# Two more PSUM banks for the products of the first two f-pairs' gate in moe2's first 512-token block

## The chip, the cores and the metric

The kernel runs on one core of a Trainium2 chip. The metric is the device time of one execution in microseconds (us); the lower the better. The work is spread over five engines with a queue each: TensorE (PE) multiplies, VectorE (DVE), ScalarE (ACT) and GpSimd (POOL) do the elementwise work, SyncE (SP) issues the DMA transfers. PE writes into PSUM, which has eight banks per partition; a bank holds 512 fp32 values. Before PE may overwrite a bank, the engine that reads the old result out of it must be done.

## What is computed

Three layers, one after the other. First, attention with a window of 128 positions, 4 batches of 8 heads, 576 positions each, 64 wide. Then two feed-forward layers on the 2304 tokens of width 512:

```python
def _moe_ref(x, w_in, w_out):          # d_ff 2048
    h = x @ w_in
    r = np.maximum(h, 0.0)
    return ((r * r) @ w_out)

def _moe2_ref(x, w_gate, w_val, w_out):  # d_ff 1536
    gate = 1.0 / (1.0 + np.exp(-(x @ w_gate)))
    val = x @ w_val
    return (gate * val @ w_out)
```

The weights come as 64-bit floats and the result is fp32. To keep the precision, each operand is split into a high and a low part of type fp32r, and a product is made of three matmuls: high by high, high by low, low by high.

## The kernel before

The kernel first lists all its operations with what each reads and writes (`plan.op`), then a planner (`Plan.schedule`) plays the list through with a cost for each operation on each engine it may run on. The order in which the planner starts the operations is the order in which they are written into the five queues. Each engine then works through its queue strictly in that order, and an instruction waits until what it depends on is done. Where an operation may run on DVE or POOL (`dve_or_pool`, line 375), the planner also chooses the engine. Buffers are slots in groups; the eight PSUM banks are the group `b`. A buffer gets its bank when its first operation is planned, and the bank comes free when the last operation that uses the buffer is done. So one operation that may start earlier or later in the plan moves all that follow it, on all engines, up to the end.

The last layer, moe2, goes over the tokens in five blocks: block 0 of 256 tokens, and blocks 1 to 4 of 512 tokens each. Block 0 is computed directly: `gv` (lines 1033 to 1035) makes gate and val into the banks `pg` and `pv`, and `o_step` (line 1062) multiplies by `w_out` into the banks `o`.

Blocks 1 to 4 use a Strassen-Winograd scheme with seven products instead of eight. For each pair of 128-wide slices of d_ff (f = 0, 2, 4, 6, 8, 10) and each of gate and val, `gv_strassen` makes the seven products P1, P2, P6, P7, P5, P4, P3, each of six matmuls of 256 columns (line 937). I call these seven products a part; a block has twelve parts: gate 0, val 0, gate 2, val 2, and so on. All parts share two PSUM buffers: P1, P6, P5 and P3 go to `pa`, and P2, P7 and P4 go to `pd`. Before the next product may go to the same bank, its result is taken out:

- P1, P6 and P5 by an ACT copy into `cg` (line 338), P7 by an ACT copy into `qc` (line 338);
- P2 and P4 by a DVE addition onto `cg` (line 953);
- P3 by an ACT sigmoid for gate (line 971), by a DVE multiplication for val (line 982).

The result of a val part is then multiplied with the gate, combined into sums (`ss`, line 995) and split into high and low parts `ah` (ACT at line 338, DVE or POOL at line 335). From these, `o_strassen` (line 1095) makes the products of the output layer, six of them into six banks `o`, in groups of three matmuls; the seventh goes through `pd` (line 1095 as well, out by line 1113). Two such calls per f-pair are spread over the parts that follow. The weights of the parts are fetched from a scratch area in HBM by SP: the tiles that hold sums (`st2`, shown as st) have five buffers, and each part needs four of them.

`xb` (called per block) loads the tokens of a block into `xf`, makes four sums of them (DVE or POOL), and splits the seven operands into high parts (ACT, line 338) and low parts (DVE, line 335).

Of the kernel before, what the change touches and what calls it, by code (L numbers as in the profile page):

```python
# [287 lines left out]
def attention_moe_moe2_kernel(ctx: ExitStack, tc, q, k, v, w_in, w_out1, w_gate, w_val, w_out2, out):  # L288
# [26 lines left out]
    TOP = {k: "t" for k in ("tq", "tk", "ts", "tp", "tv")}  # L315
    CAP = {"raw": 3, "nq": 1, "nk": 1, "qs": 1, "ks": 1, "wt": 6, "vs": 3, "st": 4, "pt": 2, "t": 3,
           "h": 2, "y": 4, "pg": 2, "pv": 2, "o": 6, "pa": 1, "pd": 1, "xacc": 2, "ob": 2, "ysg": 2, "raw2": 2, "pp": 2, "xp": 2,
           "tg": 2, "tw": 2, "st2": 5, "so": 5, "xf": 6, "cg": 4, "ss": 2, "ah": 12, "oc": 4, "qc": 3}
    CAP0 = {"nat": 2, "nq": 4, "nk": 4, "qs": 3, "qw": 3, "ks": 3, "vs": 3, "st": 5, "pt": 6, "t": 6}
    plan = Plan(SIZE, TOP)  # L320
# [3 lines left out]
    def new(kind, shape, dtype, early=False):  # L324
        g = GROUP[kind]
        t = TOP.get(kind, kind)
        cap = CAP0.get(t, CAP.get(t)) if early else CAP.get(t)
        return plan.buf(kind, g, cap, lambda slot: pools["ps" if g == "b" else "sb"].tile(
            shape, dtype, tag="%s%d" % (g, slot), name=kind, bufs=1))
# [588 lines left out]
    PAD = {}  # L918
    LATER = 2.0

    def gv_strassen(n, kind, f, e0):
        where, wts = XB[n], TW.pop((n, kind, f))
        for k in ("pa", "pd"):
            if k not in PAD:
                PAD[k] = new(k, [128, 512], F32)
        kA, kD = PAD["pa"], PAD["pd"]
        A, D = (lambda: kA()[:, :256]), (lambda: kD()[:, :256])

        def product(name, ps, start=False):
# [253 lines left out]
    for n in range(nblk):  # L1183
        e0 = endA + 3 * F2 * n
        xb(n, e0 - (14 if n == 0 else 3))
        for f in range(F2):
            e1 = e0 + 3.0 * f
            if n == 0:
                gv(n, f, e1)
                if f:  # L1190
                    o_step(0, f - 1, e1)
                continue
            if (n, f) == (1, 0):
                o_step(0, F2 - 1, e1)

            if todo and todo[0][0] <= (n - 1) * F2 + f:
                o_strassen(*todo.pop(0)[1:], e1)
            kind, f0 = ("gate", "val")[f % 2], f // 2 * 2
            sums(n, kind, f0, e1 - 9)
            gv_strassen(n, kind, f0, e1)  # L1200
            if f % 2:
                sums(n, "out2", f0, e1 - 6)
                todo += [((n - 1) * F2 + f + 2 + i, n, f0, i) for i in range(2)]
# [52 lines left out]
```

## Time and profile before

| what | value |
|---|---|
| three timed runs | 985.03, 985.9, 986.41 us, median 985.9 us |
| the profiled execution | 986.72 us, of which the span from first to last instruction is 985.0 us |
| PE busy | 963.0 us (98% of the span), 7676 matmuls |
| DVE, ACT, POOL busy | 625.0, 568.4, 218.0 us |
| mean granted TensorE clock | 0.997 of full speed |

A busy PE is not PE at its fastest. The end of a matmul is modelled (0.28 us after its start), while the next matmul starts 0.12 us after it in a dense stretch. A pause of up to 0.16 us between two matmuls is therefore still shown as busy. What PE loses is better read from the start times in the timeline, or from the number of matmuls in a stretch of fixed length, than from the busy share.

### The profile page before, as it was taken

What the parts mean: (1) busy time and instruction counts of PE and PEld (TensorE: products, weight loads), DVE (VectorE), ACT (ScalarE), POOL (GpSimd) and SP (SyncE); (2) the same over time, 40 slices, a digit from 0 to 9 for tenths busy, and PEclk for the clock granted to TensorE, in tenths of its full rate; (3) what the DMA queues carried; (4) which work ended last, traced back from release to release, by engine and by line L of the source; (5) the groups of instructions that cost most, each with busy time, mean ns of one, the idle gap of its engine ahead of it and who ended that gap; (6) DMA issues with size and microseconds to landing.
All of it is one profiled execution on the core that took longest, in us unless ns stands there. A gap on an engine that the chain in (4) does not pass through costs nothing.

```text
span 985.0 us, 21787 instructions
## 1 busy us (share of the span) xinstructions
PE 963.0 (98%) x7676; PEld 911.5 (93%) x7676; DVE 625.0 (63%) x1630; ACT 568.4 (58%) x1536; POOL 218.0 (22%) x339
## 2 busy tenths in 40 slices
PE   7899999999999999999999999999999999999997
PEld 6599989998988998998899999899999999999997
DVE  6999988777687777567621324536755485565555
ACT  7887777776677587576643423444544444454433
POOL 4611112314232223114200001102221141122121
PEclk9999999999999999999999999999999999999999
DMA  8645558656784776675689741676776677677931
GB/s 227 148 146 166 172 150 257 201 170 193 227 239 152 240 245 203 197 211 179 205 280 358 255 120 37 183 215 204 234 264 215 216 247 250 200 232 258 333 117 44
DMA packets 188140, 201.71 MB, mean 205 GB/s; under 512 B 86400, under 2 KB 119680, under 8 KB 188032
## 3 DMA queue, kind: packets, MB, share of 16 engines
q1 hardware_dynamic: 188032, 200.33, 65.0%
q8 instruction: 61, 1.00, 0.4%
q14 instruction: 47, 0.39, 0.1%
HBM read 153.09 MB, written 47.19 MB: 203 GB/s over the span
## 4 chain that ended last, share of the span: by engine, by line
PE 83%; DMA 5%; ACT 5%; DVE 4%; issue 3%; POOL 1%; SPq 0%; POOLq 0%; DVEq 0%; ACTq 0%
PE y L818 18%; PE pa L937 13%; PE pd L937 10%; PE o L1095 10%; PE h L781 6%; PE h L783 6%; PE h L782 6%; PE tv L759 3%; DMA wscr<-pp 2%; DMA raw<-in_moe_w_in_dram 2%; PE ts L637 2%; PE pd L1095 2%; PE o L1062 1%; PE tp L726 1%; PE tq L602 1%
## 5 line engine op out<-in xcount | busy, mean ns | idle before, releaser
L818 PE MATMUL y<-gs,wh 128*128 128x256 f32 (+1 forms) x1024 | 217.4, 304 | 0.0
L818 PEld LDWEIGHTS y<-gs,wh 128*128 128x128 f32 x1024 | 163.6, 190 | 9.1 <-issue 7.3
L781 PE MATMUL h<-x,wh 128*128 128x256 f32 (+1 forms) x512 | 156.2, 305 | 0.4 <-ACT qs L607 0.4
L783 PE MATMUL h<-x,wl 128*128 128x256 f32 (+1 forms) x512 | 151.2, 295 | 0.4 <-DVE wl L335 0.4
L818 PE MATMUL y<-gs,wl 128*128 128x256 f32 (+1 forms) x512 | 151.4, 296 | 0.0
L782 PE MATMUL h<-x,wh 128*128 128x256 f32 (+1 forms) x512 | 151.0, 295 | 0.0
L338 ACT ACTIVATE cg<-pa 128x256 f32<-128x256 f32 x144 | 55.1, 383 | 110.8 <-PE pa L937 94.3
L335 DVE TENSOR_TENSOR gs<-r,gs 128x320 fp32r<-128x320 f32 (+1 forms) x121 | 57.3, 473 | 74.9 <-ACT gs L338 74.6
L736 POOL TENSOR_SCALAR_AFFINE_SELECT pt<-pt 128x256 f32<-128x256 f32 (+1 forms) x144 | 67.6, 490 | 164.9 <-ACT pt L730 139.9
L781 PEld LDWEIGHTS h<-x,wh 128*128 128x128 f32 x512 | 96.7, 189 | 3.4 <-issue 2.1
L783 PEld LDWEIGHTS h<-x,wl 128*128 128x128 f32 x512 | 96.5, 188 | 0.6 <-DVE wl L335 0.6
L818 PEld LDWEIGHTS y<-gs,wl 128*128 128x128 f32 x512 | 96.9, 189 | 0.0
L782 PEld LDWEIGHTS h<-x,wh 128*128 128x128 f32 x512 | 96.6, 189 | 0.0
L795 ACT ACTIVATE r<-h 128x256 f32<-128x256 f32 (+1 forms) x128 | 51.9, 406 | 73.6 <-PE h L783 72.5
L937 PE MATMUL pa<-x,st 128*128 128x256 f32 x576 | 85.0, 283 | 1.1 <-ACT cg L338 1.0
L953 DVE TENSOR_TENSOR cg<-cg,pd 128x256 f32<-128x256 f32 x96 | 40.0, 416 | 62.9 <-ACT cg L338 58.1
L937 PEld LDWEIGHTS pa<-x,st 128*128 128x128 f32 x576 | 74.8, 189 | 1.8 <-ACT cg L338 1.7
L995 POOL TENSOR_TENSOR ss<-cg 128x256 f32<-128x256 f32 x31 | 27.4, 885 | 192.6 <-DVE cg L982 75.5
L1095 PE MATMUL o<-wr,ah 128*128 128x256 f32 x432 | 69.0, 281 | 0.2 <-DVE ah L335 0.2
L1095 PE MATMUL o<-so,ah 128*128 128x256 f32 x432 | 66.2, 281 | 0.0
L667 ACT ACTIVATE st<-st,sm 128x128 f32<-128x128 f32 x144 | 56.7, 402 | 13.4 <-DVE sm L660 13.3
L338 ACT ACTIVATE gs<-r 128x256 fp32r<-128x256 f32 (+1 forms) x128 | 56.4, 441 | 8.5 <-PE y L818 4.5
(175 smaller groups left out, 2139.7 us busy)
## 6 DMA issues: line engine op xcount, KB each, us to landing
st<-wscr SPq DMA_DIRECT2D x192, 256.0 KB, 3.9
wscr<-pp SPq DMA_DIRECT2D x72, 512.0 KB, 3.6
so<-wscr SPq DMA_DIRECT2D x96, 256.0 KB, 3.9
raw<-in_moe_w_out_dram SPq DMA_DIRECT2D x28, 512.0 KB, 4.0
wr<-wscr SPq DMA_DIRECT2D x54, 256.0 KB, 4.9
raw<-in_moe_w_in_dram SPq DMA_DIRECT2D x16, 512.0 KB, 4.8
raw<-in_moe_w_gate_dram SPq DMA_DIRECT2D x12, 512.0 KB, 4.6
raw<-in_moe_w_val_dram SPq DMA_DIRECT2D x12, 512.0 KB, 4.3
```

The lines of the kernel that those rows point to most:

```text
L335: return lambda e: eng(e).tensor_tensor(out=out(), in0=a(), in1=b(), op=ALU.subtract)
L338: return lambda e: nc.scalar.activation(out=out(), in_=in_(), func=AF.Copy, scale=scale)
L667: op({"ACT": 386}, lambda e, x=x: nc.scalar.activation(out=st()[:, x, :], in_=st()[:, x, :], func=AF.Exp, bias=sm()[:, x:x + 1], scale=-1. ...
L736: op({"POOL": pool_sel(2 * cols)}, lambda e: nc.gpsimd.affine_select(out=pt_of(what, j), in_=pt_of("own", j), pattern=[[0, 2], [1 if mine ...
L781: nc.tensor.matmul(ps()[:, :N], w[0]()[:, c], x()[:, 0, cc, :N], start=cc == 0, stop=False)
L782: nc.tensor.matmul(ps()[:, :N], w[0]()[:, c], x()[:, 1, cc, :N], start=False, stop=False)
L783: nc.tensor.matmul(ps()[:, :N], w[1]()[:, c], x()[:, 0, cc, :N], start=False, stop=cc == CC - 1)
L795: op({"ACT": act_ns(N, True)}, lambda e: nc.scalar.activation(out=g()[:, :N], in_=ps()[:, :N], func=AF.Relu), r=[ps], w=[g], prio=ep, also ...
L818: nc.tensor.matmul(y()[:, c0:c0 + N], w[a]()[:, c], gs()[:, b, :N], start=f == 0 and p == 0 and n != 1, stop=f == F1 - 1 and p == 2, skip_ ...
L937: nc.tensor.matmul(ps()[:, :256], w()[:, z * 256 + cc * 128:z * 256 + cc * 128 + 128], x, start=start and cc == 0 and i == 0, stop=cc == 1 ...
L953: op({"DVE": dve_ns(256)} if psum else dve_or_pool(256), lambda e: eng(e).tensor_tensor(out=quarter(i, j)(), in0=quarter(i, j)(), in1=src( ...
L1095: nc.tensor.matmul(o()[:, 256 * t:256 * t + 256], a_()[:, c_ + 128 * t:c_ + 128 * t + 128], w()[:, 256 * z:256 * z + 256], start=start and ...
```

## The change

In block 1 the parts are numbered 0 (gate 0), 1 (val 0), 2 (gate 2), 3 (val 2) and so on. Parts 0 and 2 write their products to two new PSUM buffers `pa2` and `pd2`; all other parts of block 1, and blocks 2 to 4, use `pa` and `pd` as before.

```diff
-             "h": "b", ..., "o": "b", "pa": "b", "pd": "b"}
+             "h": "b", ..., "o": "b", "pa": "b", "pd": "b", "pa2": "b", "pd2": "b"}
...
-           "h": 2, "y": 4, "pg": 2, "pv": 2, "o": 6, "pa": 1, "pd": 1, "xacc": 2, ...
+           "h": 2, "y": 4, "pg": 2, "pv": 2, "o": 6, "pa": 1, "pd": 1, "pa2": 1, "pd2": 1, "xacc": 2, ...
...
     def gv_strassen(n, kind, f, e0):
         where, wts = XB[n], TW.pop((n, kind, f))
-        for k in ("pa", "pd"):
+
+        ka, kd = ("pa", "pd") if n > 1 or 2 * (f // 2) + (kind == "val") not in (0, 2) else ("pa2", "pd2")
+        for k in (ka, kd):
             if k not in PAD:
                 PAD[k] = new(k, [128, 512], F32)
-        kA, kD = PAD["pa"], PAD["pd"]
+        kA, kD = PAD[ka], PAD[kd]
```

No instruction of the computation is added or removed. The two new buffers take two of the eight banks from the end of block 0 until the last product of part 2 has been read; then the banks go to `o`. The number of matmuls stays. The order of all queues is the same up to the first product of block 1 and differs from there to the end of the program. On POOL the order holds 225 rows before and 204 after, on DVE 1518 and 1540; of the splits into `ah` that are 512 wide, POOL has 4 before and 23 after.

The first place is PE in the middle of parts 0 and 1 of block 1. Before, from P4 of gate 0 on:

```order
L937 MATMUL pd<-xp,st_8129 128x256 x6
L937 MATMUL pa<-xp,wr 128x256 x6
L937 MATMUL pd<-x,wr 128x256 x6
L937 MATMUL pa<-x,wr 128x256 x6
L937 MATMUL pa<-x,st_8245 128x256 x6
L937 MATMUL pd<-x,st_8731 128x256 x6
L937 MATMUL pa<-x,st_8754 128x256 x6
L937 MATMUL pd<-xp,st_8766 128x256 x6
L937 MATMUL pa<-xp,wr 128x256 x6
```

These are P4 and P3 of gate 0, then P2, P1, P6, P7, P5, P4, P3 of val 0. P6 (the fifth row) goes to the same bank as P1 right ahead of it. Now the same place, from P3 of gate 0 on; `pa_8694` and `pd_8702` are the new buffers `pa2` and `pd2`, `pa` and `pd` without a number the old ones, and L939 is the former L937:

```order
L939 MATMUL pa_8694<-xp,wr 128x256 x6
L939 MATMUL pd<-x,wr 128x256 x6
L939 MATMUL pa<-x,st_8245 128x256 x6
L939 MATMUL pa_8694<-x,wr 128x256 x6
L939 MATMUL pd<-x,st_8740 128x256 x6
L939 MATMUL pa<-x,st_8753 128x256 x6
L939 MATMUL pd_8702<-x,wr 128x256 x6
L939 MATMUL pd<-xp,st_8774 128x256 x6
L939 MATMUL pa<-xp,wr 128x256 x6
L939 MATMUL pd<-x,wr 128x256 x6
L939 MATMUL pa<-x,wr 128x256 x6
```

Rows 2, 3, 5, 6, 8 and 9 are P2, P6, P7, P5, P4 and P3 of val 0; P1 of val 0 stands further up, as the third product of the block. Rows 4 and 7 are P1 and P2 of gate 2, and the last two rows P2 and P1 of val 2. The products of two or three parts are interleaved.

The second place is PE at the start of block 2. Before, from the seventh output product of a pair (`pd<-so,ah`) to P3 of gate 0 of block 2 and the output products behind it:

```order
L1095 MATMUL pd<-so,ah 128x256 x6
L1095 MATMUL o<-wr,ah 128x256 x3
L937 MATMUL pa<-x,wr 128x256 x6
L937 MATMUL pd<-x,wr 128x256 x6
L937 MATMUL pa<-x,st_9743 128x256 x6
L937 MATMUL pd<-x,st_9796 128x256 x6
L937 MATMUL pa<-x,st_9803 128x256 x6
L937 MATMUL pd<-xp,st_9822 128x256 x6
L1095 MATMUL o<-wr,ah 128x256 x9
L937 MATMUL pd<-x,wr 128x256 x6
L937 MATMUL pa<-xp,wr 128x256 x6
L1095 MATMUL o<-wr,ah 128x256 x3
```

The third row is P1 of block 2, and P2, P6, P7, P5, P4 follow with no output product between them; behind the nine output products stand P2 of val 0 and P3 of gate 0, and the next product to `pa`, P1 of val 0, stands right behind the last row. Now, from P1 of block 2 on:

```order
L939 MATMUL pa<-x,wr 128x256 x6
L1097 MATMUL o<-so,ah 128x256 x9
L939 MATMUL pa<-x,st_9757 128x256 x6
L1097 MATMUL o<-so,ah 128x256 x3
L1097 MATMUL pd<-so,ah 128x256 x6
L1097 MATMUL o<-wr,ah 128x256 x3
L939 MATMUL pa<-x,st_9794 128x256 x6
L1097 MATMUL o<-wr,ah 128x256 x3
L939 MATMUL pd<-x,wr 128x256 x6
L939 MATMUL pa<-xp,wr 128x256 x6
L1097 MATMUL o<-wr,ah 128x256 x3
L939 MATMUL pd<-x,st_9763 128x256 x6
```

P1, P6 and P5 now stand ahead of P2, with output products between them, and P3 and P7 follow. The products that go to `pa` run ahead of those that go to `pd` from block 1's third pair to the end.

## Rows read from the trace of the kernel before

**Rows 1.** The page: busy time by engine, and the chain that ended last
```profile
PE 963.0 (98%) x7676; PEld 911.5 (93%) x7676; DVE 625.0 (63%) x1630; ACT 568.4 (58%) x1536; POOL 218.0 (22%) x339
...
PE 83%; DMA 5%; ACT 5%; DVE 4%; issue 3%; POOL 1%; SPq 0%; POOLq 0%; DVEq 0%; ACTq 0%
```

**Rows 2.** Stretches of 20 us: busy us and (x instructions) per engine, clock, DMA
```profile
610.00:630.00 20.00, 17.77 (x140) 16.73 (x139) 12.64 (x23) 9.33 (x23) 4.73 (x5) 1.00 0.51 159
640.00:660.00 20.00, 20.00 (x171) 20.00 (x171) 9.02 (x20) 8.52 (x21) 2.25 (x3) 1.00 0.69 202
...
700.00:720.00 20.00, 19.16 (x155) 18.48 (x154) 16.30 (x31) 9.26 (x22) 8.01 (x9) 1.00 0.71 239
...
780.00:800.00 20.00, 19.15 (x160) 18.74 (x158) 14.04 (x25) 11.50 (x27) 6.07 (x5) 1.00 0.77 247
800.00:820.00 20.00, 19.99 (x168) 19.75 (x167) 12.48 (x24) 7.69 (x19) 6.49 (x8) 1.00 0.90 284
...
880.00:900.00 20.00, 18.62 (x154) 18.15 (x153) 15.14 (x27) 9.30 (x22) 9.79 (x9) 1.00 0.63 203
900.00:920.00 20.00, 20.00 (x170) 19.95 (x169) 10.89 (x23) 10.02 (x24) 3.39 (x4) 1.00 1.02 373
```

**Rows 3.** Waits of PE from 608 us on: total us, times, longest
```profile
PE pd L937 <- DVE cg L953: 3.9, 5, 1.3
PE pa L937 <- ACT cg L338: 1.0, 2, 0.5
PE o L1095 <- DVE ah L335: 0.2, 1, 0.2
```

**Rows 4.** Timeline, first block: start, us, engine, line [idle before <-releaser]
```profile
614.25 1.35 POOL L335 TENSOR_TENSOR xf<-xf 128x512 f32<-128x512 f32 x1 [3.92 <-PE o L1062]
614.37 1.78 DVE L335 TENSOR_TENSOR xf<-xf 128x512 f32<-128x512 f32 x1
...
614.69 0.88 PE L937 MATMUL pa<-xp,wr 128*128 128x256 f32 x6
...
616.08 0.41 DVE L953 TENSOR_TENSOR cg<-cg,pd 128x256 f32<-128x256 f32 x1
...
616.53 0.98 PE L937 MATMUL pd<-x,wr 128*128 128x256 f32 x6 [0.97 <-DVE cg L953]
...
617.35 0.88 PE L937 MATMUL pa<-x,wr 128*128 128x256 f32 x6
618.27 0.38 ACT L338 ACTIVATE cg<-pa 128x256 f32<-128x256 f32 x1 [1.12 <-PE pa L937]
...
618.71 0.97 PE L937 MATMUL pa<-x,st 128*128 128x256 f32 x6 [0.47 <-ACT cg L338]
```

**Rows 5.** Timeline of PE at the start of block 2
```profile
700.00 0.90 PE L937 MATMUL pa<-x,st 128*128 128x256 f32 x6
701.60 0.97 PE L937 MATMUL pd<-x,st 128*128 128x256 f32 x6 [0.70 <-DVE cg L953]
702.40 0.89 PE L937 MATMUL pa<-x,st 128*128 128x256 f32 x6
...
705.63 0.87 PE L937 MATMUL pa<-xp,wr 128*128 128x256 f32 x6
706.33 0.51 PE L1095 MATMUL o<-wr,ah 128*128 128x256 f32 x3
706.97 0.97 PE L937 MATMUL pa<-x,wr 128*128 128x256 f32 x6
```

**Rows 6.** Timeline: a wide multiplication on DVE, a wide split on POOL
```profile
635.98 0.69 DVE L982 TENSOR_TENSOR cg<-cg 128x512 f32<-128x512 f32 x1
...
914.99 1.29 POOL L335 TENSOR_TENSOR ah<-ss,ah 128x512 fp32r<-128x512 f32 x1 [2.10 <-DMA so<-wscr]
```

**Rows 7.** DMA issues from 600 to 640 us: count, KB each, median us to landing
```profile
st<-wscr SPq DMA_DIRECT2D x14, 256.0 KB, 3.0
```

More of the change, by code (lines that the diff above doesn't have):

```diff
@@ L313, in attention_moe_moe2_kernel @@
              "xf": "s", "xacc": "s", "cg": "s", "ss": "s", "ah": "s", "ysg": "s", "oc": "s", "qc": "r",
[1 row of a table removed]
[1 row of a table added]
     TOP = {k: "t" for k in ("tq", "tk", "ts", "tp", "tv")}
     CAP = {"raw": 3, "nq": 1, "nk": 1, "qs": 1, "ks": 1, "wt": 6, "vs": 3, "st": 4, "pt": 2, "t": 3,
-           "h": 2, "y": 4, "pg": 2, "pv": 2, "o": 6, "pa": 1, "pd": 1, "xacc": 2, "ob": 2, "ysg": 2, "raw2": 2, "pp": 2, "xp": 2,
+           "h": 2, "y": 4, "pg": 2, "pv": 2, "o": 6, "pa": 1, "pd": 1, "pa2": 1, "pd2": 1, "xacc": 2, "ob": 2, "ysg": 2, "raw2": 2, "pp": 2, "xp": 2,
            "tg": 2, "tw": 2, "st2": 5, "so": 5, "xf": 6, "cg": 4, "ss": 2, "ah": 12, "oc": 4, "qc": 3}
```

2 rows, old and new, of the table GROUP are left out of this document.

## The prediction

> **What bounds the kernel now.** I read the page first [rows 1]: PE is busy for 98% of the span, and 83% of the chain that ended last is PE. So only what PE itself does or waits for counts. The clock is at full speed in the stretches that matter (the column behind POOL reads 1.00 in [rows 2], the higher of its two levels, 2.4 GHz), so it is no term here.
>
> The busy share hides short pauses, since the modelled end of a matmul lies 0.28 us after its start. So next I counted matmuls in stretches of 20 us over blocks 1 to 4 [rows 2]. A clean stretch holds 171 (640 to 660), which is 20 / 171 = 0.117 us for a matmul. Five stretches hold fewer: 140 at the start of block 1, 155 at the start of block 2, 160 and 168 at that of block 3, 154 at that of block 4. The deficits are 31 + 16 + 11 + 3 + 17 = 78 matmuls, and 78 x 0.117 = 9.1 us. The rest of the four blocks runs at 170 to 172 in a stretch.
>
> Then the waits [rows 3]: what PE waits for is nearly always a bank. For `pd` it is the DVE addition that takes out P2 or P4, for `pa` the ACT copy. No transfer is among them.
>
> The timeline shows the price of a bank that is reused too soon. A group of six matmuls takes 0.71 us from start to next start. At 617.35 P1 goes to `pa`, and P6 right behind it goes to `pa` too [rows 4]: P6 starts at 618.71, 1.36 us later instead of 0.71. The steps are 0.88 until the last matmul is through, 0.04 to the start of the ACT copy, 0.38 for the copy, 0.06 to PE. So a bank is free again about 0.65 us after PE could have gone on, and with a DVE addition (0.41, [rows 4]) 0.69. After a wait, the first group needs 0.82 instead of 0.71 (616.53 to 617.35), which is 0.10 more for each wait.
>
> From this follows a rule to read an order by: count the matmuls that stand between two products in the same bank. Six (0.71 us) just cover the reading; three (0.355) leave 0.30, with the restart 0.4; none leaves 0.65, with the restart 0.75. The case of three is in [rows 5]: P3 to `pa` at 705.63, three output matmuls at 706.33, the next product to `pa` at 706.97 instead of 706.68. And six are enough only while DVE or ACT come at once. At 616.53 and 701.60 they did not: P2 waited 1.84 - 0.71 = 1.13 us [rows 4], and P7 of block 2 waited 1.60 - 0.71 = 0.89 [rows 5]. In the first case DVE sat 1.78 us in one subtraction, which POOL's subtraction, begun 0.12 us earlier, held up; the addition came only behind it, at 616.08.
>
> **The change, step by step.** The new banks themselves cost nothing: no matmul, copy or addition is added. `pa2` and `pd2` take two banks that `pg` and `pv` have left, and give them back before the six `o` banks are all wanted.
>
> What counts is the order, and in it the distance between products in one bank. In the whole PE order before, of 358 such pairs 2 have none between them, 4 have three and 37 have six; the others have nine or more. In the new order, of 356 pairs none has less than six, 8 have six, the others nine or more. The reason is the alternation that the order shows: a product to `pa`, three output matmuls, a product to `pd`. It begins in block 1 because two parts can be under way at once, and the planner keeps it to the end, because `pa` runs ahead and `pd` behind. With `pd` behind, the copy that the DVE addition adds onto is always there when the product is done.
>
> Terms of the gain, against the profiled execution of 986.72 us:
> - All deficits of the five stretches: 9.1 us. To this I add the fourth pair with three between, which lies in the last block's last part (0.4). Together 9.5 us that could go. In it are the two pairs with none (2 x 0.75 = 1.5) and the four with three (4 x 0.4 = 1.6), which the order removes for certain; the other 6.4 us are waits at distances of six or more, where DVE or ACT came late.
> - What comes back for certain: in block 1, P3 of val 0 is followed by P2 of val 2 and then by P1 of val 2 to the same bank. P3 of a val part is read by a DVE multiplication, and the DVE order puts P4's addition and the 512-wide multiplication (0.69, [rows 6]) ahead of it. From the end of P4 that is 0.21 + 0.41 + 0.69 + 0.41 + 0.06 = 1.78 us, and PE has P3 and P2 to do, 1.42. Left are 0.36, with the restart 0.46.
> - One pair in `pd` with six between is read by DVE (P4 of val 0, then P2 of val 2): between 0 and 1.23 us, what the same pair costs before (1.13 and 0.10). It is nearer to the lower end, since the addition has no POOL subtraction ahead of it; I take 0.3.
> - The three starts of a block. DVE has its burst of splits there as before. Between P4 of the old part, the seventh output product and P2 of the new block there is now room, so the wait of 0.89 + 0.10 = 1.0 has no place of its own, but other additions follow at a distance of nine, with 0.38 us to spare. Between 0 and 1.0 for each; with nothing nearer, I take the middle, 3 x 0.5 = 1.5.
> - The end of the program: the last output products wait for the last split in both orders, with the same 24 matmuls between. Nothing changes.
>
> Sum: 9.5 - 0.46 - 0.3 - 1.5 = 7.2 us. The execution of 986.72 becomes 979.5; the median of the three runs is 0.8 lower than that execution, so I predict 985.9 - 7.2 = 978.7. With the lower bounds of what comes back (0 for all) it is 976.4, with the upper ones (0.46 + 1.23 + 3.0 = 4.7, a gain of 4.8) 981.1.
>
> **Rivals.**
> - The gain ends with block 1. The waits at the three block starts may come from DVE's burst of splits (16.3 of 20 us busy at 700 to 720, [rows 2]) and not from the distance; then they come back in the new order at another product. Only the first stretch gains: 31 x 0.117 - 0.46 - 0.3 = 2.9, so 983.0. For it speaks that the distance there was six, where in other places six cost nothing; against it that the order has no six there any more.
> - Slower, through POOL. Of the splits into `ah` that are 512 wide, 23 go to POOL instead of 4. One holds POOL for 1.29 us [rows 6], and a DVE subtraction that meets it waits it out, as at 614.37 [rows 4]; an addition queued behind it then keeps `pd`. If each meeting costs 1.23, six of the 19 new ones eat up the gain of 7.2, and ten make 12.3 - 7.2 = 5.1 more, 991.0. For it: the one clear meeting in [rows 4]. Against it: the split at 914.99 lies in a stretch of 170 matmuls [rows 2, 6], so it cost PE nothing, and in POOL's order most of the new ones stand between the block starts.
> - No change, since something else holds PE at the same pace. Three parts under way want their weights sooner, through five buffers. P5 of val 0 can be fetched once P7 of gate 0 is done, after five groups, and is needed after fourteen: 9 x 0.71 = 6.4 us for a fetch that lands after 3.0 [rows 7]. At 900 to 920 the DMA queues are full (share 1.02), and PE still does 170 matmuls [rows 2]. If transfers took back all of it, the time would stay at 985.9. The Trainium skill (TensorE: Matmul & The Clock Gate, HAM oscillation — how this bites in real kernels) reports of a kernel whose loop had been reordered that "Adding PSUM double-buffering gave no further gain". By that rule nothing would change here either and the time would be 985.9; the trace does not bear it out, since here PE's waits name the bank's reader [rows 3].
>
> **How the numbers follow.** Forecast 0.76, gain ends with block 1 0.12, no change 0.07, slower through POOL 0.05. The forecast's own range is 976.4 to 981.1. To leave out no more than 2 in 10 I take in the first rival: 976.4 to 983.2. About 0.2%, or 2 us, is what a measurement of this kernel can tell from no change. The forecast lies beyond that with its whole range, the first rival mostly (0.11 of 0.12). So faster 0.87, same 0.08, slower 0.05.
>
> **What would show it.** In the changed kernel's trace: the stretch of 20 us from the first product of block 1 should hold 160 matmuls or more, and those at the block starts 166 or more. The waits of PE for DVE's addition should fall from 3.9 us to about 1. One wait of about 0.4 us should stand ahead of P1 of val 2 in block 1. Waits of PE for `st` tiles would show the third rival right, stretches of fewer than 165 matmuls in the middle of blocks beside wide POOL splits the second. The prediction is wrong in its main step if the block starts still miss more than ten matmuls each.

## The result, and the profile after

| | kernel before | changed kernel |
|---|---|---|
| timed, median (lowest to highest) | 986.15 us (985.03 to 987.03) | 976.04 us (975.76 to 976.71) |
| ratio to before | | 0.9907, 95% interval 0.9894 to 0.992 |
| timed again beside other kernels | 985.74 us | 975.63 us, ratio 0.9901 (0.9885 to 0.9917) |
| profiled execution, its span | 986.72, 985.0 us | 976.05, 974.3 us |

The change saves 10.1 us by the medians, 9.2 by the ratio. Forecast were 978.7 us and a gain of 7.2, with a range from 976.4 to 983.2. The sign and, in the main, the mechanism fit the numbers below; the gain was forecast 2 to 3 us too small, and the median of 976.04 lies 0.4 us beyond the range's lower end (the ratio on the 985.9 us shown before gives 976.7, just inside).

Of the profiled difference of 10.7 us, 1.0 has nothing to do with the change. Up to the first product of block 1 the order is the same in both kernels, and yet this product starts at 608.69 before and at 607.68 after. In the profiles of all the kernels below, it starts between 605.74 and 608.69. So from here on I compare the time from the first product of block 1 to the last group of output matmuls, both read from the timeline of one execution. I call it the PE stretch. First the timeline of the kernel before (start, us, engine, line, operation):

```profile
608.69 0.88 PE L937 MATMUL pa<-x,wr 128*128 128x256 f32 x6
...
978.50 0.86 PE L1095 MATMUL o<-wr,ah 128*128 128x256 f32 x6
```

And that of the changed kernel:

```profile
607.68 0.88 PE L939 MATMUL pa<-x,wr 128*128 128x256 f32 x6
...
967.80 0.87 PE L1097 MATMUL o<-wr,ah 128*128 128x256 f32 x6
```

That is 369.81 and 360.12 us: the change is worth 9.69 us. The changed kernel's profile from the second timed comparison gives 360.12 again, so this measure repeats far better than the time of a whole execution. Of the kernel before there is one profile.

The page after, which answers to [rows 1]: PE does the same 7676 matmuls and has a larger share of the chain that ended last (91% instead of 83%).

```profile
PE 959.1 (98%) x7676; PEld 910.7 (93%) x7676; DVE 626.7 (64%) x1653; ACT 571.0 (59%) x1537; POOL 205.0 (21%) x315
...
PE 91%; DVE 3%; ACT 2%; DMA 1%; issue 1%; SPq 0%; POOL 0%; POOLq 0%; DVEq 0%; ACTq 0%
```

PE's busy time fell by only 3.9 us of the 10, since up to 0.16 us of each pause counts as busy. The matmuls per stretch tell more; the stretches after that answer to [rows 2]:

```profile
610.00:630.00 20.00, 19.84 (x165) 19.48 (x163) 11.40 (x23) 11.36 (x28) 3.83 (x5) 1.00 0.57 172
...
700.00:720.00 20.00, 20.00 (x170) 20.00 (x169) 14.60 (x28) 9.46 (x23) 6.67 (x6) 1.00 0.75 237
...
780.00:800.00 20.00, 20.00 (x172) 20.00 (x171) 16.82 (x31) 10.05 (x24) 8.43 (x9) 1.00 0.86 277
800.00:820.00 20.00, 20.00 (x170) 20.00 (x170) 11.91 (x25) 9.68 (x24) 3.01 (x3) 1.00 0.76 249
...
880.00:900.00 20.00, 20.00 (x170) 20.00 (x169) 12.20 (x25) 8.16 (x20) 5.88 (x6) 1.00 0.84 272
```

Where 140, 155, 160, 168 and 154 matmuls stood, there are now 165, 170, 172, 170 and 170. At 780 to 800 DVE is busy for 16.82 of 20 us, and PE runs without a gap. (The stretches lie at fixed times, and the changed kernel reaches block 3 some 5 us sooner: before, the same burst of DVE shows in the stretch from 790 to 810, with 17.44.) Of PE's waits [rows 3], the 3.9 us for DVE's addition and the 1.0 us for ACT's copy are gone; these two are left:

```profile
PE o L1097 <- DVE ah L335: 0.2, 1, 0.2
PE pa L939 <- DVE cg L984: 0.2, 1, 0.2
```

The second is the predicted wait ahead of P1 of val 2. In the timeline after, from P3 of val 0 on:

```profile
619.99 0.88 PE L939 MATMUL pa<-xp,wr 128*128 128x256 f32 x6
...
620.71 0.94 PE L939 MATMUL pd<-x,wr 128*128 128x256 f32 x6
620.72 0.69 DVE L984 TENSOR_TENSOR cg<-cg 128x512 f32<-128x512 f32 x1
621.33 0.42 DVE L984 TENSOR_TENSOR cg<-pa,cg 128x256 f32<-128x256 f32 x1
...
621.80 0.98 PE L939 MATMUL pa<-x,wr 128*128 128x256 f32 x6 [0.16 <-DVE cg L984]
...
622.62 0.88 PE L939 MATMUL pa<-x,st 128*128 128x256 f32 x6
```

P2 starts at 620.71, 0.72 after P3: no wait ahead of it, though its six matmuls take 0.94 instead of 0.88, 0.06 more. P1 starts 1.09 after P2 instead of 0.71, and the group behind it 0.82 later: 0.38 + 0.11 = 0.49 us, of which 0.06 is P2's own and 0.43 the wait of P1, where 0.46 was forecast. The view of waits shows 0.2 of that, because it counts from the modelled end of the matmul before.

Why the starts of blocks cost nothing shows at block 2. First the kernel before, ahead of the rows of [rows 5]: POOL's subtraction, two splits of the new block's operands on DVE, P2 of gate 0, and the addition that reads it:

```profile
698.77 1.28 POOL L335 TENSOR_TENSOR xf<-xf 128x512 f32<-128x512 f32 x1
699.03 2.18 DVE L335 TENSOR_TENSOR x<-xf,x 128x512 fp32r<-128x512 f32 x2
699.28 0.87 PE L937 MATMUL pd<-x,wr 128*128 128x256 f32 x6
...
701.13 0.41 DVE L953 TENSOR_TENSOR cg<-cg,pd 128x256 f32<-128x256 f32 x1
```

The product was through at 700.15 and the addition came at 701.13, 0.98 late: the two splits took 2.18 us beside POOL's subtraction, where two such splits take 1.28 when nothing meets them (shown below, in the run without POOL). P7, the next product to `pd`, had only P6's six matmuls ahead of it and waited.

Now the changed kernel: a subtraction on POOL beside a multiplication on DVE, then P2, P7 and P4 of gate 0 and P2 of val 0 of the new block:

```profile
691.11 1.31 POOL L335 TENSOR_TENSOR xf<-xf 128x512 f32<-128x512 f32 x1
...
691.82 1.15 DVE L984 TENSOR_TENSOR cg<-cg 128x512 f32<-128x512 f32 x1
...
696.43 0.87 PE L939 MATMUL pd<-x,wr 128*128 128x256 f32 x6
...
697.34 0.42 DVE L955 TENSOR_TENSOR cg<-cg,pd 128x256 f32<-128x256 f32 x1 [0.20 <-PE pd L939]
...
698.20 0.87 PE L939 MATMUL pd<-x,st 128*128 128x256 f32 x6
...
699.99 0.87 PE L939 MATMUL pd<-xp,st 128*128 128x256 f32 x6
700.05 1.29 DVE L335 TENSOR_TENSOR ah<-ss,ah 128x512 fp32r<-128x512 f32 x2
...
701.26 0.41 DVE L955 TENSOR_TENSOR cg<-cg,pd 128x256 f32<-128x256 f32 x1
...
702.48 0.88 PE L939 MATMUL pd<-x,wr 128*128 128x256 f32 x6
```

POOL and DVE still meet: the 512-wide multiplication takes 1.15 us instead of 0.69 [rows 6] (1.10 and 1.06 at the starts of blocks 3 and 4). But it reads no bank, and no product to `pd` is due: from P4 of the old part (690.41) to the seventh output product (694.29) stand 27 matmuls. P2 of gate 0 now comes behind P1, P6 and P5, when the splits of the new block's operands are done. DVE is idle, and the addition starts at 697.34, 0.04 after the product is through. From P2 to P7 there are nine matmuls (698.20 - 696.43 = 1.77 us, less 0.71 for P2 itself), where before there were six.

One addition does come late, the one onto P4: the product was through at 700.86, and two splits kept DVE until 701.26. But the next product to `pd`, P2 of val 0, is wanted only at 702.48, and the bank was free at 701.67. From P4 to P2, PE has 702.48 - 699.99 = 2.49 us between the starts, less 0.71 for P4 itself: 15 matmuls, where before there were nine. At the starts of blocks 3 and 4 the distances are the same, nine and 15, the addition onto P2 again starts at once (0.03 and 0.04 after the product), and the one onto P4 is 0.41 late.

### The profile page after: what moved, and what is told of

Same layout as the page of the kernel before. It is cut to its first block, busy times and chain, and to the rows that moved or that the text cites. A ratio compares the mean times of both kernels' runs of the same rounds, so it can differ in the third digit from the quotient of the medians.

```text
span 974.3 us, 21742 instructions
## 1 busy us (share of the span) xinstructions
PE 959.1 (98%) x7676; PEld 910.7 (93%) x7676; DVE 626.7 (64%) x1653; ACT 571.0 (59%) x1537; POOL 205.0 (21%) x315
## 4 chain that ended last, share of the span: by engine, by line
PE 91%; DVE 3%; ACT 2%; DMA 1%; issue 1%; SPq 0%; POOL 0%; POOLq 0%; DVEq 0%; ACTq 0%
PE y L818 21%; PE pa L939 14%; PE pd L939 10%; PE o L1097 10%; PE h L781 7%; PE h L783 6%; PE h L782 6%; PE tv L759 3%; PE ts L637 2%; PE o L1064 2%; PE pd L1097 2%; PE tp L726 1%; PE tq L602 1%; ACT st L667 1%; PE ts L630 1%
## 5 line engine op out<-in xcount | busy, mean ns | idle before, releaser
L939 PE MATMUL pa<-x,st 128*128 128x256 f32 x576 | 84.0, 281 | 0.0
L939 PEld LDWEIGHTS pa<-x,st 128*128 128x128 f32 x576 | 74.9, 189 | 0.0
L1097 PEld LDWEIGHTS o<-wr,ah 128*128 128x128 f32 x432 | 59.4, 189 | 0.4 <-DVE ah L335 0.4
```

Source lines behind the costliest of these rows:

```text
L939: nc.tensor.matmul(ps()[:, :256], w()[:, z * 256 + cc * 128:z * 256 + cc * 128 + 128], x, start=start and cc == 0 and i == 0, stop=cc == 1 ...
L1097: nc.tensor.matmul(o()[:, 256 * t:256 * t + 256], a_()[:, c_ + 128 * t:c_ + 128 * t + 128], w()[:, 256 * z:256 * z + 256], start=start and ...
```

## The experiments

Each was run beside the kernel before on the same chip; its median differs a little from one comparison to the next (985.19 to 986.15 us), so the ratios compare better than the medians. The PE stretch is from each kernel's own profile; in the kernel before it is 369.81 us.

| kernel | PE stretch, us | against before | median, us | ratio to before (95%) |
|---|---|---|---|---|
| changed kernel, two profiles | 360.12, 360.12 | -9.69 | 976.04, 975.63 | 0.9907 (0.9894 to 0.992), 0.9901 (0.9885 to 0.9917) |
| gate 0 only | 368.28 | -1.53 | 982.99 | 0.9976 (0.9966 to 0.9985) |
| val 0 only | 367.67 | -2.14 | 982.67 | 0.9973 (0.9962 to 0.9983) |
| gate 2 only | 360.46 | -9.35 | 975.44 | 0.9902 (0.9886 to 0.9919) |
| val 2 only | 361.82 | -7.99 | 976.35 | 0.9915 (0.99 to 0.993) |
| before's order without POOL | 368.21 | -1.60 | 984.01 | 0.9993 (0.9982 to 1.0004) |
| changed, wide splits on DVE | 360.03 | -9.78 | 974.91 | 0.9894 (0.9879 to 0.9908) |
| changed, 24 pairs at distance three | 370.67 | +0.86 | 984.9 | 0.9997 (0.9987 to 1.0007) |
| changed, two multiplications swapped | 359.68, 359.72 | -10.13, -10.09 | 973.98, 975.88 | 0.9887 (0.9872 to 0.9903), 0.99 (0.9884 to 0.9916) |
| swapped, and wide splits on DVE | 359.73 | -10.08 | 975.59 | 0.9897 (0.9881 to 0.9913) |

### Which part's banks do it

Theory: the new banks help inside block 1, and beyond it only because they leave the products to `pa` ahead of those to `pd`, a phase that the planner keeps to the end. Rival: the room that the two banks give in block 1 does it all. Four kernels give the new banks to one part of block 1 only:

```diff
-        ka, kd = ("pa", "pd") if n > 1 or 2 * (f // 2) + (kind == "val") not in (0, 2) else ("pa2", "pd2")
+        ka, kd = ("pa", "pd") if n > 1 or 2 * (f // 2) + (kind == "val") not in (0,) else ("pa2", "pd2")
```

and with `(2,)`, `(1,)` and `(3,)` in place of `(0,)` for gate 2, val 0 and val 2.

> Only part 0 (gate 0) of block 1 uses the second pair of banks. In the planned PE order, distances in one bank below six: one pair with none between (P1, P6 of gate 2) and four with three (at the starts of blocks 2, 3, 4 and in the last part), as in the kernel before but for one pair with none; pa does not run ahead of pd. Theory (the gain is the distances, kept to the end by the order): block 1 saves the pair with none (0.75) and the wait at P2 of val 0 (1.23), blocks 2 to 4 nothing: 2.0 us below the kernel before, some 984.1. Rival (two banks help where they are used, each part about half of the gain): about half of the way to the changed kernel, 981.

> Only part 2 (gate 2) of block 1 uses the second pair. In the planned PE order one pair has none between (P1, P6 of val 0), none has three; from block 1's third pair on the order alternates as in the changed kernel. Theory: block 1 keeps 0.75 at that pair, 1.23 at P2 of val 0 and 0.46 ahead of P1 of val 2, and so saves only some 1.2 of its 3.6 us; the starts of blocks 2 to 4 (5.5 us) and the last part (0.4) are saved: some 7.1 us below the kernel before, 979.0. Rival (half of the gain for one of two parts): 981.

> Only part 1 (val 0) of block 1 uses the second pair, the one part that does not use it in the changed kernel. Planned PE order: no pair with none between, but the four with three as in the kernel before; pa does not run ahead of pd in blocks 2 to 4. Theory: block 1 is rid of its waits (3.6 us), blocks 2 to 4 pay theirs as before (47 matmuls, 5.5 us, missing at the three block starts): some 982.5. Rival (each part that uses the pair gives about half): 981, with the block starts changed as well.

> Only part 3 (val 2) of block 1 uses the second pair. Planned PE order: both pairs with none between are there in block 1 as in the kernel before, none has three, and from block 1's third pair on the order alternates as in the changed kernel. Theory: block 1 saves nothing (its stretch of 20 us misses about 30 matmuls), the block starts and the last part save 5.9 us: some 980.2. With the val 0 kernel this is the other half of the gain: the two savings should add up to that of the changed kernel, 10 us. Rival (half for each part): 981, with block 1 at half of its loss and the block starts at half of theirs.

The kernels fall into two classes. With gate 0 alone or val 0 alone, some 2 us are gained; with gate 2 alone or val 2 alone, nearly all. In stretches of 20 us, gate 0 only:

```profile
610.00:630.00 20.00, 19.22 (x156) 18.58 (x155) 10.79 (x22) 10.58 (x26) 3.87 (x4) 1.00 0.50 163
...
700.00:720.00 20.00, 19.39 (x158) 18.74 (x157) 15.37 (x28) 9.16 (x22) 8.24 (x9) 1.00 0.72 228
```

and val 2 only:

```profile
610.00:630.00 20.00, 18.75 (x151) 17.98 (x150) 11.34 (x24) 10.45 (x26) 3.86 (x4) 1.00 0.49 157
...
700.00:720.00 20.00, 20.00 (x170) 19.99 (x170) 15.28 (x30) 10.15 (x24) 6.50 (x6) 1.00 0.80 268
```

Gate 0 only does better in the first block (156 against 151) and still pays at the starts of blocks 2 to 4, as before the change (158 matmuls at 700, 157 at 780, 153 at 880; before 155, 160 and 154). Val 2 only gets no new bank before the fourth part, keeps more than half of the loss in block 1 (20 of 31 matmuls), and runs clean from block 2 on. The timeline at the start of block 2 shows the difference. Gate 0 only has P2 and P7 close together, with P6 alone between them, and P7 waits for the addition, as before:

```profile
695.91 0.84 PE L939 MATMUL pd<-x,wr 128*128 128x256 f32 x6
...
697.76 0.41 DVE L955 TENSOR_TENSOR cg<-cg,pd 128x256 f32<-128x256 f32 x1
...
698.23 0.98 PE L939 MATMUL pd<-x,st 128*128 128x256 f32 x6 [0.71 <-DVE cg L955]
```

In val 2 only, P3 to `pa` follows P2 at once, since P1, P6 and P5 are done by then, and an output group stands ahead of P7, as in the changed kernel:

```profile
698.53 0.87 PE L939 MATMUL pd<-x,wr 128*128 128x256 f32 x6
...
699.24 0.87 PE L939 MATMUL pa<-xp,wr 128*128 128x256 f32 x6
...
700.31 0.87 PE L939 MATMUL pd<-x,st 128*128 128x256 f32 x6
```

So two parts of the gain are told apart. The kernels do the same number of matmuls, so the time from the first product of block 1 to the 250th matmul behind it (33.4 us before) is what block 1 costs. It is 2.0 us shorter in gate 0 only, 2.6 in val 0 only and gate 2 only, 1.4 in val 2 only, and 3.0 in the changed kernel. From there to the end, gate 2 only, val 2 only and the changed kernel win another 6.8, 6.6 and 6.7 us; gate 0 only and val 0 only lose 0.4 to 0.5 again. In these two a split on POOL holds up an output group once (0.5 and 0.4 us in the view of waits). The two parts don't need each other.

My expectations missed in size. Gate 2 only was expected at 979.0 and came out at 975.4, level with the changed kernel; val 2 only at 980.2, and it came out at 976.4. In gate 2 only, block 1 holds 160 matmuls in the stretch at 610 us, 20 more than before, though gate 0 and val 0 have the old banks. The wait of P2 of val 0 [rows 4] came in none of the four. I had booked it as one that only the banks of gate 0 remove. It hung on something else: before, POOL has one of the two subtractions on `xf` at this place, and DVE's takes 1.78 us beside it; in the four kernels and in the changed one DVE does both, in 0.68 to 0.69 us each. In gate 2 only and val 2 only, P4 of gate 0 and P2 of val 0 share a bank as before; there these 1.2 us went with the planner's other choice of engine, and not through a bank.

### POOL, from both sides

Theory: the order decides, and which engine does the work does not matter. First, in the changed kernel, the 23 splits into `ah` of 512 columns that POOL has are moved to DVE at the same place in the order:

```diff
+    for o in plan.order:
+        if o.eng == "POOL" and o.on == dve_or_pool(512) and any(b.kind == "ah" for b in o.bufs):
+            o.eng = "DVE"
```

> The changed kernel with its planned order kept, but the 23 splits into ah, 512 wide, that the planner had given to POOL run on DVE at the same place in the order (in the kernel before POOL had 4). No distance between two products in a bank changes. Theory (distances): PE's waits stay away or come back only where a split of 0.69 us stands ahead of an addition at a distance of nine, which leaves 0.38 us: between 976 and 978. Rival (a good part of the gain comes from the other share of work between DVE and POOL): with the splits back on DVE at least 3 us come back, 979 or more.

The PE stretch is 360.03 us, 0.09 less. In this order the splits on POOL cost PE nothing, which is the end of the rival "slower through POOL" for the changed kernel; nor do they save anything. (The time of 974.91 us lies below the 976 to 978 expected, but the interval of its ratio overlaps that of the changed kernel.)

Second, the kernel before, with all of POOL's 86 operations from block 1 on moved to DVE, so that no subtraction on DVE can meet one on POOL:

```diff
+    begun = next(i for i, o in enumerate(plan.order) if any(x.kind == "pa" for x in o.bufs))
+    for o in plan.order[begun:]:
+        if o.eng == "POOL" and "DVE" in o.on:
+            o.eng = "DVE"
```

> The kernel before with its planned order kept, but all 86 additions and subtractions that POOL does from block 1 on run on DVE at the same place in the order. The distances stay: two pairs with none between, four with three, 37 with six. It asks how much of the waits at distance six is POOL holding up DVE. Theory (the distance is the cause, and whatever DVE has in its queue decides how much late it comes): the wait at P2 of val 0 gets shorter by up to 0.5, those at the block starts stay as they are since POOL's work is now in DVE's queue: 984 to 988. Rival (POOL's hold on DVE is the cause): the waits for DVE's addition go, 4 us or more below the kernel before, 981 or less.

Two of its stretches, at the starts of blocks 1 and 2:

```profile
610.00:630.00 20.00, 18.99 (x156) 18.57 (x156) 12.15 (x26) 10.13 (x25) 0.00 (x0) 1.00 0.52 173
...
700.00:720.00 20.00, 19.12 (x155) 18.41 (x154) 17.87 (x37) 8.93 (x21) 0.00 (x0) 1.00 0.72 229
```

The loss in block 1 shrinks from 31 matmuls to 15, because the subtraction that POOL held up there [rows 4] is quick now. The stretches at 700 and 880 lose as much as before (155 and 155, where 155 and 154 stood). But they lose it at other places. Two splits of the new block's operands on DVE and P7 of gate 0, then P2 and P7 of gate 2 further on:

```profile
696.17 1.28 DVE L335 TENSOR_TENSOR x<-xf,x 128x512 fp32r<-128x512 f32 x2
...
697.86 0.98 PE L937 MATMUL pd<-x,st 128*128 128x256 f32 x6
...
712.69 0.98 PE L937 MATMUL pd<-x,wr 128*128 128x256 f32 x6 [0.46 <-DVE xacc L1113]
...
715.75 0.98 PE L937 MATMUL pd<-x,st 128*128 128x256 f32 x6 [0.29 <-DVE cg L953]
```

The two splits take 1.28 us instead of 2.18, and P7 of gate 0 waits less than 0.1 us instead of 0.89, at the same distance of six. So the wait that the prediction read in [rows 5] was POOL's hold on DVE as well. In its place come waits of 0.62 and 0.45 us at P2 and P7 of gate 2, though 12 and 15 matmuls lie between them and the last product to `pd`: DVE now has POOL's work too (17.87 of 20 us). In PE's waits, those for the addition fall from 3.9 us to 0.8, and 1.1 for the seventh product's reader appear. At the 250th matmul 1.9 us are won, over the whole PE stretch 1.6, so nothing behind block 1. The run does not tell what the old order would cost if POOL's work were done elsewhere at no cost to DVE; so at the block starts it is not settled how much of the loss was the distance of six and how much POOL's hold. The theory holds for the changed order; in the old one POOL's share decides which products wait.

### The distance by itself

To measure what three matmuls between two products in a bank cost, the changed kernel was made worse: 12 times in block 2, the product to `pa` that stands behind a product to `pd` is put ahead of it. The row "product to `pa`, three output matmuls, product to `pd`, product to `pa`" becomes "product to `pa`, three output matmuls, product to `pa`, product to `pd`", which brings both banks to a distance of three, 24 pairs in all. In the edit, `ib` is the place of the product to `pd` and `ic` that of the product to `pa` behind it.

```diff
+            plan.order.insert(ib, plan.order.pop(ic))
```

> The changed kernel, but in block 2 twelve products to pa are moved ahead of the product to pd in front of them, all else in its order. This makes 24 pairs of products in one bank with three matmuls between (12 in pa, 12 in pd) where there were none. Theory: each leaves 0.30 us open and costs 0.10 at the restart, 24 x 0.40 = 9.6 us, all of it in block 2: 985.6, and block 3 stays as it is. Rival (distances matter only where DVE or ACT are busy, as at the block starts): 2 us or less.

The PE stretch grows from 360.12 to 370.67 us: 10.55 / 24 = 0.44 us for each pair, forecast 0.40. In time the whole gain of the change is gone (984.9 us). One of the stretches of block 2:

```profile
720.00:740.00 20.00, 18.69 (x142) 17.06 (x142) 7.55 (x17) 7.41 (x18) 1.29 (x1) 1.00 0.46 150
```

DVE and ACT are less busy at 720 to 740 (7.55 and 7.41 of 20 us) than anywhere in the changed kernel's rows above, and PE does 142 matmuls: here it is not their load that costs, it is the distance. At 780, behind the edit, there are 172 again. One pair from the timeline, P4 to `pd`, three output matmuls, the next product to `pd`:

```profile
734.19 0.87 PE L940 MATMUL pd<-xp,st 128*128 128x256 f32 x6
...
734.89 0.51 PE L1099 MATMUL o<-wr,ah 128*128 128x256 f32 x3
...
735.09 0.42 DVE L957 TENSOR_TENSOR cg<-cg,pd 128x256 f32<-128x256 f32 x1 [2.11 <-PE pd L940]
...
735.57 0.98 PE L940 MATMUL pd<-x,wr 128*128 128x256 f32 x6 [0.16 <-DVE cg L957]
...
736.38 0.52 PE L1099 MATMUL o<-wr,ah 128*128 128x256 f32 x3
```

DVE was idle and started at once. The output group takes 0.68 to the next start instead of 0.355, and the next product 0.81 instead of 0.71: 0.33 + 0.10 = 0.43 us. And PE's waits in this kernel, for the additions and the copies:

```profile
PE pd L940 <- DVE cg L957: 2.2, 10, 0.5
PE pa L940 <- ACT cg L338: 0.5, 3, 0.2
```

The view names the two readers, but only 13 of the 24 waits and 2.7 of the 10.55 us.

### The wait that was left

In the changed kernel, the multiplication that reads P3 out of `pa` stands on DVE behind the 512-wide one, which reads no bank. This kernel swaps the two in block 1's first val part (`wide` is the 512-wide one, `first` the one that reads `pa`); it also writes the program's last sum into the buffer of P4, to free its last store from another wait:

```diff
+    wide, first = MULT[1, 0, 1, 0], MULT[1, 0, 0, 1]
+    plan.order.remove(first)
+    plan.order.insert(plan.order.index(wide), first)
...
-        op(dve_or_pool(512), lambda e: ...(out=v(), in0=v(), in1=o["P4"](), op=ALU.add), ..., w=[v], ...)
-        store(v, 1, 0)
+        op(dve_or_pool(512), lambda e: ...(out=o["P4"](), in0=v(), in1=o["P4"](), op=ALU.add), ..., w=[o["P4"]], ...)
+        store(o["P4"], 1, 0)
```

> The changed kernel with two more edits. First, in block 1 the DVE multiplication that reads P3 of val 0 stands ahead of the 512-wide one, so that P1 of val 2 finds its bank free: 0.44 us less. Second, the last addition of a block's output (v and P4) writes into P4's buffer instead of v's, so that it need not wait for the sum that reads v; at the end of the program the last store then hangs on DVE's last sum (970.24) instead of POOL's addition (971.05): up to 0.8 us less. Together 1.2 us: 974.8. Rival (the end hangs on the last matmul and the chain of sums on DVE whatever POOL does): 975.6.

The timeline at the place shown above, after the swap:

```profile
619.12 0.94 PE L940 MATMUL pd<-x,wr 128*128 128x256 f32 x6
619.32 0.42 DVE L985 TENSOR_TENSOR cg<-pa,cg 128x256 f32<-128x256 f32 x1 [0.29 <-PE pa L940]
...
619.90 0.88 PE L940 MATMUL pa<-x,wr 128*128 128x256 f32 x6
...
620.62 0.88 PE L940 MATMUL pa<-x,st 128*128 128x256 f32 x6
```

P1 now starts 0.78 after P2, not 1.09, and the next group follows at 0.72. The PE stretch is 0.44 us shorter. Not all of that is this wait: at the 250th matmul the swapped kernel is only 0.27 ahead, since a new pause of 0.16 us comes a little later (at the group at 623.91), and the rest gathers in small steps up to the end. The other half failed: the end is not sooner. From the start of the last output group to the end of the span it takes 972.3 - 965.79 = 6.5 us, in the changed kernel 974.3 - 967.80 = 6.5. The stores leave SP one behind the other, and the freed one (968.17) is not the last: another follows at 968.68. What the end hangs on was not traced further.

The median of 973.98 us looked like 2 us less than the changed kernel's, but in this profile block 1 began at 606.11 instead of 607.68, before anything that differs. So the two were compared once more on one chip, with a third that has both the swap and the splits on DVE:

> The changed kernel again, unaltered, so that the next two are compared with it on one chip. Expected is its earlier ratio to the kernel before, 0.9907 (0.9894 to 0.992), some 976 us where the kernel before takes 985.3.

> The kernel with the multiplication that reads pa moved ahead of the wide one, and the last sum written into P4's buffer. Theory: the one wait of 0.44 us in block 1 is gone and nothing else differs, so the time lies 0.4 us below that of the changed kernel in the same call. Rival: the 2 us by which it was faster in the earlier call are its own, then it is 2 us below. If the order of the two multiplications were worth nothing, the two would be level.

> The kernel of the run above, with the 512-wide splits into ah on DVE instead of POOL as well. Theory: POOL's share of them costs PE nothing and gains nothing, so the time is that of the run above within 0.5 us. Rival: the 1 us by which the changed kernel with these splits on DVE came out below the changed kernel is real, since no DVE instruction meets a wide POOL split any more; then it is 1 us below the run above.

Timed, the three are level: 975.63, 975.88 and 975.59 us. The 2 us were not the kernel's. The PE stretch tells the swap's share again: 360.12 for the changed kernel, 359.72 with the swap, 359.73 with both, so 0.40 us, and nothing for the splits. A version that beats the changed kernel in time by more than can be measured was not found.

## Why the prediction was right in kind and too small in size

- **The bound** (PE, and in it the waits for banks) held. The clock column reads 1.00 in all stretches shown of both kernels, so the gain is matmuls that start sooner.
- **What could go, 9.5 us.** The deficits of the five stretches and the fourth pair. The PE stretch gained 9.69, and 0.49 came back at P2 and P1 of val 2 in block 1 and 0.2 at P7 of its first part (610.61, which PE began 0.82 after the product before it and left again after 0.80). So 10.4 us went, not 9.5. The trace of the kernel before has them: the steps of over 0.15 us from one matmul's start to the next add up to 10.7 us beyond the usual 0.118 (in the changed kernel 1.5), and only 0.46 of that is the wait at the very end, which both have. The counts of matmuls resolve one in each stretch, five times 0.117 us, and miss short pauses outside the five.
- **What comes back in block 1.** P1 of val 2: 0.46 forecast, 0.43 in the timeline. P2 of val 2: 0.3 forecast, 0.06 measured.
- **The starts of the three blocks: the term that was mis-sized.** "Between 0 and 1.0 for each; with nothing nearer, I take the middle, 3 x 0.5 = 1.5." It was 0: the stretches hold 170, 172 and 170 matmuls. The distance of nine was read rightly, from P2 to P7 of gate 0, but the addition there starts 0.04 us after the product, behind the burst of splits and not in it. The addition that does come 0.4 late has 15 matmuls behind its product. I priced all additions by the shortest distance of the new order, nine with 0.38 us to spare, and did not ask which of them stands behind a split. PE's and DVE's orders were there to be read; how late DVE would be was not in them.
- **The sum.** 7.2 + 1.5 (block starts) + 0.3 (P1 and P2 of val 2) + 0.9 (more to lose than counted) - 0.2 (P7) = 9.7. That is the PE stretch's gain; the medians give 10.1 and the ratio 9.2 (7.9 to 10.5). The lower end of the range, 976.4, let nothing come back, but took the 9.5 for certain; it had no room for more to lose than was counted.
- **The cause of the late additions: half seen.** The prediction found POOL's hold on DVE at P2 of val 0, and put the block starts down to a distance of six and to DVE's burst. The trace shows the same hold there: two splits take 2.18 us at 699.03, 2.21 at 790.59 and 2.74 at 881.87, each behind a subtraction that POOL began some 0.25 us earlier.
- **The phase.** That the gain in blocks 2 to 4 comes with `pa` running ahead was argued from the order. It is shown now: gate 2 only and val 2 only have the phase and win 9.35 and 7.99 us, gate 0 only and val 0 only have banks without it and win 1.53 and 2.14. What in the phase does it is read from the rows above (the wider distances, and P2 coming behind the burst of splits), and the two were not tested apart. Why the planner falls into the one phase or the other was not traced.
- **"The gain ends with block 1"** (0.12) was wrong for this change. It names something real, though: it is just what gate 0 only and val 0 only do. That their times (982.99 and 982.67) meet its 983.0 so closely is luck: their PE stretch is 1.53 and 2.14 us shorter, not 2.9, and the kernel before was faster on that chip. The cause that it names, DVE's burst of splits, is there in both orders and hardly smaller in the new one (16.82 of 20 us at 780, before 17.44 from 790 on), but in the new one no product to `pd` waits behind it.
- **"Slower through POOL"** (0.05): moving the 23 splits away changes the PE stretch by 0.09 us. **"No change"** (0.07): PE's waits name no transfer, and at 900 to 920, with the queues nearly as full as before (0.98 instead of 1.02), PE does 171 matmuls. The sentence of the Trainium skill (TensorE: Matmul & The Clock Gate, HAM oscillation — how this bites in real kernels) on double-buffered PSUM would have meant 985.9; this kernel's trace does not agree with it, by 9.7 us, since here the bank's reader was what PE waited for.
- **What would show it:** all five signs came. First stretch 165 (160 or more), block starts 170 to 172 (166 or more), the waits for DVE's additions 0 (about 1), one wait of 0.4 ahead of P1 of val 2, and no wait for an `st` tile.

## What to carry to other kernels

Where an engine's queue is fixed, count the work between two uses of one buffer in the queue's order, and compare it with the time that the reader needs. Six matmuls just covered a read here when the reader came at once, three cost 0.44 us each time, and 15 absorbed a reader that came 0.4 us late; in the run without POOL, a fuller DVE made PE wait even behind 12 and 15. So ask for each read what the reader has in its own queue at that moment, and whether another engine holds it up there. A small change at one place can move a periodic schedule into another phase that lasts to the end of the program, so look at what follows before pricing only the place that was edited. And measure inside one trace, between two events that the change encloses: that repeated to 0.04 us here (360.12 twice; 359.68 and 359.72), where medians of four to six executions of one kernel differed by up to 2 us.

## What the runs showed that was not expected

- The view of waits shows only a part of short pauses: 2.7 of 10.55 us where 24 pauses of 0.44 us were put in. In the kernel before it shows 4.9 us [rows 3] of what became a gain of 9.7.
- The same instructions up to block 1 took between 605.74 and 608.69 us in 13 profiled executions. This is larger than several of the effects that were studied.
- Without POOL, DVE did everything from block 1 on in the kernel before, with 17.87 of 20 us busy at 700, and PE's stretch became shorter by 1.6 us, not longer. The waits at the block starts did not go, they moved to other products.
